# One op list for attention tail, mixing, transition and MLP, with the first block's LayerNorm inside the mixing

## The chip, the cores and the metric

The kernel runs on one core of one Trainium2 chip. Times are device microseconds of one execution, from the first instruction to the last on that core, with inputs and outputs in device memory. The profile is one execution of the same program, taken by the hardware profiler; its engines are PE (TensorE matmul), PEld (TensorE weight load), DVE (VectorE), ACT (ScalarE), POOL (GpSimd) and SP (SyncE, which here issues most DMAs).

## The reference

Three stages over batch 8, sequence 576, model width 512 (8 heads of 64).

```
phi(x)  = exp(+-(x @ w_phi - max|x @ w_phi|))                    # 2 x 128 features
attn    = phi(q) (phi(k)^T v) / (phi(q) sum_s phi(k) + 1e-6)      # per head, not causal
x       = attn, heads side by side                               # [8, 576, 512]
gate    = sigmoid(sum_k conv_w[k] * x[s - 4 + k])                 # 5 taps, causal
x2      = (gate * (x @ w_val)) @ w_out
u       = x2 + Re(FFT over width of (FFT over sequence of x2))
un      = (u - mean(u)) / sqrt(var(u) + 1e-6)                     # over width
out     = u + relu(un @ w_ch1) @ w_ch2                            # 512 -> 2048 -> 512
```

All in float32; each matmul is done as three matmuls of rounded high and low parts ("hi" and "lo"), and the two matrices of the MLP in a seven-product scheme (sums and differences of quarter blocks), whose sums of weight blocks are formed in the kernel and kept in a scratch array, `w_scr`.

## The kernel before

**Attention** is written by hand as steps (`run_attention`, L1281): step st projects piece st of q and k, and later stages of earlier pieces follow at fixed lags. Its last pieces end with a chain DVE `xs` (the normalised output), PE transposes `xt` (L336), ACT copy `xT`, a store to `x_scr` and a load of `xf`, one [512, 576] array for each batch. In the last steps (L1339 to L1342) the first batch's value products, `emit_V(0, m)` for four column chunks m, are written in.

**Mixing** goes batch by batch (L1359 to L1382), in the order in which the framework's scheduler puts it. For each batch: `split_x` (L433) makes hi on ACT and lo on POOL of the input (`xh`); `emit_V` (L465) makes a chunk: four tap multiply-adds on DVE (`acc`), sigmoid on ACT, 24 matmuls `val`, gating on DVE, the even and odd parts `gs`, hi on ACT and lo on POOL (`ge`). `emit_W` (L493) multiplies by w_out (`x2p`, 96 matmuls a batch), forms `fs` and its hi (ACT) and lo (DVE). `emit_FD` (L522) is the transform over width (tables `ft`, 39 matmuls), `emit_SD` (L563) the one over the sequence (tables `sq`, `sr`, 30 matmuls); its sums go into a tile `eo`, and from that DVE makes one half of u and POOL the other, and SP stores u to `u_scr`. Value products of batch b+1 run between the output products of batch b. `sum_w` (L359) loads weight blocks, forms their sums on POOL and stores them.

**The transition.** The last V chunk of batch 7 ends the written mixing. What is left of batches 6 and 7, the first MLP weights (`wr`, split into `w`), the LayerNorm of the first block (`ln_stages`, L767: sums `s`, `mean` by a matmul of ones, `A` minus mean, squares `T`, square root, reciprocal, `A` times `s`) and the MLP operands `un` are noted as ops (`note_last`, L1066) with the whole MLP (`note_mlp`, L1105).

**The planner.** `place_ops` (L1147) takes the noted ops with their dependences, gives each a duration from a small cost table, a due time from the order of the matmuls, and lets the ready op with the earliest due time go first on each engine. An op marked "vp" goes to DVE or POOL, whichever the planner finds free in time. Ops are marked old, any or new: tiles of the mixing are closed after the last old op and those of the MLP's first products (`x0`, `y`, `z`, `c11`, ...) opened after it, so that no MLP product runs before the last op of batch 7. All planned instructions carry line L59, that of the helper through which they are issued, as do the hi and lo splits and matmuls of the written part.

Of the kernel before, what the change touches and what calls it, by code (L numbers as in the profile page):

```python
# [1 line left out]

# [44 lines left out]
def resolve(x):  # L47
    return x.get() if isinstance(x, Late) else x
# [14 lines left out]
def attention_moe_mixer_kernel(  # L63
# [73 lines left out]

    base = pool(ctx, "base", 1)
# [38 lines left out]
    R = "right"  # L177
    wv_p = pool(gx, "wv", 1, side=R)
# [180 lines left out]
    def sum_w(n):  # L359
        for k in ((0, 1) if n == 0 else (n + 1,)):  # L360
            if k < len(wsteps):
                i, j, o = wsteps[k]
                wsum[k] = t = P["ws"].tile([128, 512], F32, tag="ws", name="ws")
                nc.sync.dma_start(out=t, in_=w_scr[i][j, o][:, 0:512])
        i, j, o = wsteps[n]
        t = wsum.pop(n)
        a21, a11, a12, a22 = (t[:, k * 128:(k + 1) * 128] for k in range(4))
        tt = nc.gpsimd.tensor_tensor
        tc.keep_in_program_order(tt(out=a22, in0=a21, in1=a22, op=ALU.add))
        tt(out=a21, in0=a11, in1=a21, op=ALU.subtract)  # L370
        tt(out=a11, in0=a22, in1=a11, op=ALU.subtract)
        tt(out=a12, in0=a12, in1=a11, op=ALU.subtract)
        nc.sync.dma_start(out=w_scr[i][j, o][:, 512:1024], in_=t)
# [26 lines left out]
    def open_mix():  # L400
        P["g0"] = pool(gx, "g0", 1, side=R)
        P["ws"] = pool(vx, "ws", 2, side=R)
        P["psv"] = pool(vx, "psv", 2, PSUM, side=R)
        P["psa"] = pool(vx, "psa", 1, PSUM, side=R)

    def open_mix2():
        P["x2"] = pool(mx, "x2", 1)
        P["fs"] = pool(mx, "fs", 1)
        P["ps"] = pool(mx, "ps", 4, PSUM)
        one = pool(mx, "one", 1)  # L410
        P["xr"] = [one.tile([128, NE], F32R, name=f"xr{i}") for i in range(2)]
        P["rem"] = [one.tile([128, NL], F32R, name=f"rem{a}") for a in range(2)]
        P["c256"] = one.tile([128, 5, 128], F32R, name="c256")
        P["r256"] = one.tile([97, 2, NE], F32, name="r256")
        for t in (*P["xr"], *P["rem"], P["c256"], P["r256"]):
            nc.gpsimd.memset(f32(t), 0.0)

    wsteps = [(i, j, o) for j in range(NJ) for i in range(2) for o in range(2)]
    wsum = {}
    xf = {}  # L420
    xhl = {}
    geo = {}
    x2 = {}
    fhl = {}
    yhl = {}

    def load_x(b):
        t = P["xf"].tile([128, 4, S + 4], F32, tag="xf", name="xf")
        nc.vector.memset(t[:, :, 0:4], 0.0)
        nc.sync.dma_start(out=t[:, :, 4:], in_=x_scr[b].rearrange("c p s -> p c s"))  # L430
        xf[b] = t

    def split_x(b, chunks=range(4)):  # L433
        if b not in xhl:
            xhl[b] = tuple(P["xh"].tile([128, 4, S], F32R, tag=f"x{i}", name="xh") for i in range(2))
        h, l = xhl[b]
        for c in chunks:
            hi_act(h[:, c], xf[b][:, c, 4:])
            lo_pool(l[:, c], xf[b][:, c, 4:], h[:, c])

    taps = {}

    def tap_steps(b, m):
        x = xf[b]
        if "psa" in P:
            acc = P["psa"].tile([128, 2, 512], F32, tag="pa", name="acc")[:, :, 0:HS]
        else:
            acc = P["g"].tile([128, 2, HS], F32, tag="acc", name="acc")

# [12 lines left out]
    def emit_taps(b, m):
        drain(tap_steps(b, m))

    def emit_V(b, m):  # L465
        h, l = xhl[b]
        if m == 0:
            geo[b] = tuple(P[f"g{b % 2}"].tile([128, 4, 2, NE], F32R, tag=f"g{i}", name="ge") for i in range(2))
        if (b, m) not in taps:
            emit_taps(b, m)  # L470
        t = taps.pop((b, m))
        acc = P["g"].tile([128, S], F32, tag="sg", name="sg")
        nc.scalar.activation(out=acc.rearrange("p (a s) -> p a s", a=2), in_=t, func=ACTF.Sigmoid)
        gv = P["g"].tile([128, NE], F32, tag="gv", name="gv")
# [12 lines left out]
        hi_act(gh[:, m], gs)
        lo_pool(gl[:, m], gs, gh[:, m])
        if m == 3:
            xhl.pop(b)  # L490
            xf.pop(b)

    def emit_W(b, c):  # L493
        gh, gl = geo[b]
        if b not in x2:
            x2[b] = P["x2"].tile([128, 4, 2, NE], F32, tag="x2", name="x2")
            fhl[b] = tuple(P["x2"].tile([128, 2, 2, NE], F32R, tag=f"f{i}", name="fh") for i in range(2))
        t = x2[b]
        for a in range(2):
            p = P["ps"].tile([128, NE], F32, tag="ps", name="x2p")  # L500
            for kk in range(4):
                ws = slice(c * 128, (c + 1) * 128)
                mm3(p, (wo[0][:, kk, ws], wo[1][:, kk, ws]), (gh[:, kk, a], gl[:, kk, a]), kk == 0, kk == 3)
            nc.scalar.activation(out=t[:, c, a, :], in_=p, func=ACTF.Copy)
            if c == 2 and a == 0:
                r = P["xr"][b % 2]
                hi_act(r[0:1, :], p[0:1])
                lo_dve(r[32:33, :], p[0:1], r[0:1, :])
            if c >= 2:
                if a == 0:  # L510
                    fs = P["fs"].tile([128, 2, NE], F32, tag="fs", name="fs")
                nc.vector.tensor_tensor(out=fs[:, a], in0=t[:, c - 2, a], in1=p, op=(ALU.add, ALU.subtract)[a])
# [972 lines left out]
```

## Time and profile before

| | us |
|---|---|
| median of three runs | 1389.01 (1388.45 to 1394.43) |
| profiled execution | 1393.84 |
| its span | 1391.9 |
| attention, up to 316.5 | 316.5 |
| attention tail, to 356.3 | 39.8 |
| mixing, batches 0 to 5 and the last V and W chunks, to 589.3 | 233.0 |
| transition, to the last sequence product | 44.7 |
| to the first MLP block's full pace at 658.9 | 24.9 |
| rest of the MLP | 733.0 |

The stages are cut where the trace's matmuls change name. Read it by stage: in each, the share of PE's busy time tells whether the matrix engine or something else sets the pace; the mean over the whole span hides this. Idle time in brackets behind an instruction is that of its engine just before it, with what released it.

### The profile page before, as it was taken

The page shows a single profiled execution, that of the slowest core. Times are in us where ns is not written, and L with a number is a line of the kernel's source. Part 1 is how long each engine was busy: PE and PEld are TensorE (multiplying, and loading weights), DVE is VectorE, ACT ScalarE, POOL GpSimd, SP SyncE. Part 2 cuts the span into 40 slices and gives each one's busy share as a digit, 9 for nine tenths or more (in the row PEclk, how much of TensorE's full clock was granted, in tenths as well). Part 3 has the DMA queues.
Part 4 walks back from the last instruction along what each step waited for, and adds up shares of the span by engine and source line. Part 5 has one row for each costly group of instructions (what it writes and reads, how often), then busy time and mean ns, then how long its engine had stood idle before and what let it go on. Part 6 is the DMA issues. An engine that isn't in the chain of part 4 may idle for free.

```text
span 1391.9 us, 35060 instructions
## 1 busy us (share of the span) xinstructions
PE 1335.0 (96%) x14672; PEld 1293.5 (93%) x14672; DVE 1177.5 (85%) x1989; ACT 816.8 (59%) x1549; POOL 609.0 (44%) x475
## 2 busy tenths in 40 slices
PE   7999999997999999977999999999999999999998
PEld 6888888987999999967999999999999999999998
DVE  6999998885889898788899999999888778777776
ACT  6888888863555545474555555655565455444542
POOL 3978888612577667533542243442313111111110
PEclk9999999998999999987999999999999999999999
DMA  6477877640344343245423233222533122222211
GB/s 244 156 276 261 280 265 259 223 166 26 107 152 158 134 142 111 88 161 204 131 85 121 92 121 101 89 91 86 167 115 118 63 68 84 89 64 91 91 48 45
DMA packets 89851, 186.98 MB, mean 134 GB/s; under 512 B 10455, under 2 KB 37335, under 8 KB 87518
## 3 DMA queue, kind: packets, MB, share of 16 engines
q1 hardware_dynamic: 88488, 181.33, 38.2%
q10 hardware_dynamic: 1206, 3.41, 0.6%
q8 instruction: 115, 1.88, 0.5%
q14 instruction: 42, 0.34, 0.1%
HBM read 121.79 MB, written 62.93 MB: 133 GB/s over the span
## 4 chain that ended last, share of the span: by engine, by line
PE 73%; DVE 15%; POOL 3%; issue 3%; ACT 3%; DMA 2%; SPq 0%; ACTq 0%; DVEq 0%; POOLq 0%
PE x L59 14%; PE cx L59 13%; PE y L59 7%; PE cy L59 6%; PE val L59 5%; PE x2p L59 5%; PE kv L59 4%; PE cz L59 4%; PE pj L59 3%; PE z L59 3%; PE nm L59 3%; DVE y L244 2%; PE yt L294 2%; DVE m L241 2%; DVE s L59 2%
## 5 line engine op out<-in xcount | busy, mean ns | idle before, releaser
L59 PE MATMUL cx<-h,w 128*128 128x256 f32 x1260 | 173.6, 284 | 0.0
L59 PEld LDWEIGHTS cx<-h,w 128*128 128x128 f32 x1260 | 161.9, 192 | 0.4 <-DVE acc L59 0.2
L59 DVE TENSOR_TENSOR acc<-cx,acc 128x512 f32<-128x512 f32 x144 | 99.0, 688 | 36.6 <-PE cx L59 35.7
L59 POOL TENSOR_TENSOR un<-A,un 128x512 fp32r<-128x512 f32 x38 | 49.2, 1302 | 173.2 <-ACT un L59 169.6
L59 PE MATMUL x<-un,w 128*128 128x256 f32 x864 | 118.0, 287 | 4.4 <-ACT c L59 2.3
L59 PE MATMUL val<-xh,wv 128*128 128x290 f32 x768 | 119.4, 305 | 1.3 <-DVE gv L481 0.6
L59 ACT ACTIVATE h<-z 128x512 fp32r<-128x512 f32 x108 | 64.4, 597 | 93.5 <-DVE z L59 92.8
L454 DVE SCALAR_TENSOR_TENSOR acc<-xf,cw,acc 128x576 f32<-128x576 f32 x128 | 105.1, 821 | 13.5 <-ACT acc L452 12.3
L59 PE MATMUL cy<-h,w 128*128 128x256 f32 x792 | 115.1, 282 | 1.2 <-DVE h L59 1.2
L59 PEld LDWEIGHTS x<-un,w 128*128 128x128 f32 x864 | 110.9, 195 | 5.1 <-ACT c L59 2.8
L59 PEld LDWEIGHTS val<-xh,wv 128*128 128x128 f32 x768 | 110.4, 195 | 3.2 <-POOL xh L59 1.4
L59 PEld LDWEIGHTS cy<-h,w 128*128 128x128 f32 x792 | 105.0, 191 | 1.4 <-DVE h L59 1.4
L59 PE MATMUL kv<-vraw,ke 128*64 128x66 f32 x2560 | 96.3, 228 | 3.1 <-DMA vraw<-in_v_dram 1.5
L59 PEld LDWEIGHTS kv<-vraw,ke 128*64 128x64 f32 x2560 | 84.0, 140 | 14.5 <-ACT qe L297 1.6
L241 DVE TENSOR_REDUCE m<-pj 128x8 f32<-128x1024 f32 (+1 forms) x80 | 88.6, 1107 | 9.6 <-PE pj L59 9.6
L59 POOL TENSOR_TENSOR un<-T,un 128x512 fp32r<-128x512 f32 x40 | 52.9, 1323 | 99.6 <-ACT un L59 99.6
L59 PE MATMUL x2p<-ge,wo 128*128 128x290 f32 x672 | 95.2, 296 | 0.0
L59 PE MATMUL pj<-wp,kqraw 64*128 64x128 f32 x1152 | 89.0, 292 | 5.5 <-DMA kqraw<-in_k_dram 4.4
L59 PEld LDWEIGHTS x2p<-ge,wo 128*128 128x128 f32 x672 | 91.8, 189 | 0.0
L59 PEld LDWEIGHTS pj<-wp,kqraw 64*128 64x128 f32 x1152 | 73.4, 193 | 19.1 <-issue 18.9
L244 DVE TENSOR_TENSOR y<-pj,m 128x1024 f32<-128x1024 f32 (+1 forms) x80 | 88.7, 1108 | 0.4
L59 PE MATMUL nm<-kvT,qe 128*64 128x65 f32 x2304 | 84.0, 225 | 4.8 <-DVE xs L323 2.7
(217 smaller groups left out, 3568.1 us busy)
## 6 DMA issues: line engine op xcount, KB each, us to landing
raw<-in_w_ch_dram SPq DMA_DIRECT2D x16, 1024.0 KB, 5.1
wr<-w_scr SPq DMA_DIRECT2D x32, 448.0 KB, 4.0
vraw<-in_v_dram SPq DMA_DIRECT2D x16, 660.0 KB, 9.1
x_scr<-xT SPq DMA_DIRECT2D x32, 288.0 KB, 2.8
xf<-x_scr SPq DMA_DIRECT2D x8, 1152.0 KB
out_dram<-acc SPq DMA_DIRECT2D x36, 256.0 KB, 2.2
kqraw<-in_k_dram SPq DMA_DIRECT2D x15, 576.0 KB
kqraw<-in_q_dram SPq DMA_DIRECT2D x15, 576.0 KB, 9.4
```

The lines of the kernel that those rows point to most:

```text
L59: return lambda *a, **k: f(*(resolve(x) for x in a), **{n: resolve(x) for n, x in k.items()})
L241: nc.vector.tensor_reduce(out=m, in_=pv, axis=AX.X, op=ALU.max, apply_absolute_value=True)
L244: nc.vector.tensor_tensor(out=y, in0=pv, in1=m.unsqueeze(3).to_broadcast([128, 2, 2 * n, F]), op=ALU.subtract)
L294: nc.tensor.transpose(t[:, h, j, :], y[:, h, n + j, :], ident)
L454: nc.vector.scalar_tensor_tensor(out=acc, in0=shifted(t), scalar=cw[:, m, t:t + 1], in1=acc, op0=ALU.mult, op1=ALU.add)
```

## The change

The last pieces of attention, the whole mixing, the transition and the MLP are now noted as one list of ops, and the planner places all of it. The two phases become five stages 0 to 4, each of which closes some pools of tiles and opens others; every key (tile) has a first and a last stage, and an op's stage follows from the keys that it reads and writes. The tiles of the MLP's first products (`x0`, `y`, `mean`, `c11`, `c12`, `c22`, the weights `w0`, `un`) open with stage 3, beside the last batches, where five PSUM banks go round for the mixing (six before).

```diff
     def run_attention():
...
-            for st in range(TOT + 6):
+            for st in range(TOT + 1):
...
-                if 1 <= st - TOT < 5:
-                    emit_V(0, st - TOT - 1)
...
+            note_mix()
+            note_mlp()
+            place_ops()
...
+    STAGES = {k: (a, b) for a, b, n in (
+        (0, 0, "early"), (0, 1, "att tr nm"), (0, 2, "xf xh sg"), (1, 2, "pv pa gv gs ws ge0"), (1, 3, "ge1"),
+        (2, 3, "x2 f Y fs u u256 xr rem c256 r256 ps T0 sh0 sl0"), (3, 4, "mean w0 sh sl T wr un c11 c12 c22 x0 y"),
+        (4, 4, "x1 z cx cy cz h acc w1"),
+    ) for k in n.split()}
```

The LayerNorm of the first block needs u of batch 0 alone; its load and its ops are now noted after batch 4. It takes its own tiles `T0`, `sh0`, `sl0`, and its mean a bank of the mixing's ring. Its last step, `prep_un(0)`, is noted at the end of the mixing.

```diff
+    def note_mix():
...
+        tail = note_tail()
+        next(tail)
+        for m in range(4):
+            note_taps(0, m)
+            note_V(0, m)
+            next(tail, None)
+        for b in range(NB - 1):
+            note_x(b + 1)
+            for i, c in enumerate((0, 2, 1, 3)):
+                if i < 3:
+                    note_taps(b + 1, i)
+                    note_V(b + 1, i)
+                note_W(b, c)
+                add_sums(1)
...
+            note_FD(b)
+            note_SD(b)
+            if b == 4:
+                load_a(0, u_scr)
+                ln_stages(0, K["ln0"])
+        b = NB - 2
         drain(prep_w(0, 0, K["w0"]))
         drain(prep_w(0, 1, K["w0"]))
-        ln_stages(0, K["ln0"])
-        phase[0] = "old"
-        note_FD(b, f, y, ring)
-        note_W(b + 1, geo[b + 1], xb, f, ring)
-        note_SD(b, x2[b], y, ring)
...
+        note_FD(b)
+        for c in (0, 2, 1, 3):
+            note_W(b + 1, c)
+        note_SD(b)
+        drain(prep_w(0, 2, K["w"]))
+        note_FD(b + 1)
+        note_SD(b + 1)
         prep_un(0, K["un0"])
```

In the mixing the engines of some ops change: the lo of `xh`, of `ge` and the weight sums may go to DVE or POOL (before: POOL); the lo of `fs` goes to POOL (before: DVE); the sums of the sequence products are formed in place in `x2`, so that there is no `eo`; both halves of u may go to either engine (before: one each); u is stored by ACT's queue (before: SP's in the written mixing).

```diff
-            lo_pool(l[:, c], xf[b][:, c, 4:], h[:, c])
+                o_lo("vp", l, x, h, S, [("xf", b % 2), ("xh", c, 0)], [("xh", c, 1)])
-        lo_pool(gl[:, m], gs, gh[:, m])
+        o_lo("vp", gl, gs, gh, 2 * NE, gk + [("ge", g, m, 0)], [("ge", g, m, 1)])
-        tt(out=a21, in0=a11, in1=a21, op=ALU.subtract)
+        o_tt("vp", a21, a11, a21, ALU.subtract, 128, [k11, k21], [k21])
-            lo_dve(fl[:, c0], fs, fh[:, c0])
+            o_lo(K["t_lo"], f[1][:, c0], fs, f[0][:, c0], 2 * NE, fk + [("f", c0, 0)], [("f", c0, 1)])
```

`K["t_lo"]` is "p" (POOL) as before; only the last batch used it then.

On DVE at the first block's LayerNorm, before: reciprocals, the product `A` times `s`, the low operands `un`, then the sums `eo` of batch 6.

```order
L59 RECIPROCAL s_9173<-s_9173 128x128
L59 TENSOR_TENSOR A<-A,s_9173 128x2x256 x4
L59 TENSOR_TENSOR T_9177<-A 128x512
L59 TENSOR_TENSOR T_9179<-A 128x512
L59 TENSOR_TENSOR un_1_9183<-A,un_0_9182 128x512
L59 TENSOR_TENSOR un_1_9185<-A,un_0_9184 128x512
L59 TENSOR_TENSOR un_1_9191<-T_9177,un_0_9190 128x512
L59 TENSOR_TENSOR un_1_9187<-A,un_0_9186 128x512
L59 TENSOR_TENSOR T_9177<-A,T_9177 128x512
L59 TENSOR_TENSOR wg_9201<-wr_9180,wg_9201 128x896
L59 TENSOR_TENSOR un_1_9193<-T_9177,un_0_9192 128x512
L59 TENSOR_TENSOR eo<-x_8880,ps_9205 128x290 x2
```

Now, at the same `un` operands of block 0 (here the reciprocals and the product `A` times `s` stand far above, among batch 6's ops): `un`, the differences `fs` of batch 7 (`x2b` is its array), then the sums of batch 6, in place in `x2` (here `x_6103`).

```order
L62 TENSOR_TENSOR un_1_8871<-T_8856,un_0_8870 128x512
L62 TENSOR_TENSOR un_1_8865<-T_8854,un_0_8864 128x512
L62 TENSOR_TENSOR fs<-x2b,ps_6123 128x290
L62 TENSOR_TENSOR fs<-x2b,ps_6124 128x290
L62 TENSOR_TENSOR wg_8872<-wr_8855,wg_8872 128x896
L62 TENSOR_TENSOR x_6103<-x_6103,ps_8831 128x2x290
L62 TENSOR_TENSOR x_6103<-x_6103,ps_6121 128x290 x2
L62 TENSOR_TENSOR x_6103<-x_6103,ps_6122 128x2x290
L62 TENSOR_TENSOR x_6103<-x_6103,ps_6123 128x290 x2
L62 TENSOR_TENSOR wg_8873<-wr_8857,wg_8873 128x896
```

The reciprocals and products have left this place; `fs` of batch 7 and the sums of batch 6 come right behind the operands.

On PE at the end of the mixing, before: the last sequence products of batch 7 (`sq`, `sr`) come ahead of the first MLP product, `x` from `un` and `w`.

```order
L59 MATMUL ps_9204<-sq,Y 128x290 x6
L59 MATMUL ps_9204<-sr,rem_6025 128x290
L59 MATMUL ps_9205<-sq,Y 128x290 x6
L59 MATMUL ps_9205<-sr,rem_6024 128x290 x2
L59 MATMUL ps_9206<-sq,Y 128x290 x6
L59 MATMUL ps_9206<-sr,rem_6025 128x290
L59 MATMUL x_9649<-un_0_9182,w_0_0_0_9169 128x256
L59 MATMUL x_9649<-un_1_9183,w_0_0_0_9169 128x256
L59 MATMUL x_9649<-un_0_9182,w_0_0_1_9170 128x256
```

Now the first MLP product (`x_8839`) stands between batch 6's sequence products and the width transform (`ft`) of batch 7; here its last rows.

```order
L62 MATMUL x_8839<-un_1_8859,w_1_0_0_8845 128x256
L62 MATMUL x_8839<-un_0_8858,w_1_0_1_8846 128x256
L62 MATMUL x_8839<-un_0_8858,w_1_1_0_8847 128x256
L62 MATMUL x_8839<-un_1_8859,w_1_1_0_8847 128x256
L62 MATMUL x_8839<-un_0_8858,w_1_1_1_8848 128x256
L62 MATMUL ps_6124<-ft_140,f_6109 128x258
L62 MATMUL ps_6124<-ft_141,f_6109 128x258
L62 MATMUL ps_6124<-ft_140,f_6115 128x258
```

One product of the MLP, 12 matmuls, has moved ahead of batch 7's two transforms.

On POOL in the attention tail, before: the lo of the first batch's input, the clearing of the mixing's small tiles, and four more lo of the next batch's input behind three lo of `ge`.

```order
L59 TENSOR_TENSOR xh<-xf,xh 128x576 x4
L416 MEMSET xr_6022 128x290
L416 MEMSET xr_6023 128x290
L416 MEMSET rem_6024 128x258
L416 MEMSET rem_6025 128x258
L416 MEMSET c_6026 128x640
L416 MEMSET r_6027 97x580
L59 TENSOR_TENSOR ge<-gs,ge 128x580 x3
L59 TENSOR_TENSOR xh<-xf,xh 128x576 x4
L59 TENSOR_TENSOR ge<-gs,ge 128x580 x2
L369 TENSOR_TENSOR ws<-ws 128x128
```

Now, at the lo of the next batch's input: weight sums (`ws`), two lo of `ge`, and two lo of the input.

```order
L62 TENSOR_TENSOR ws_5767<-ws_5767 128x128
L62 TENSOR_TENSOR ws_5763<-ws_5763 128x128
L62 TENSOR_TENSOR ws_5767<-ws_5767 128x128
L62 TENSOR_TENSOR ge<-gs,ge 128x580 x2
L62 TENSOR_TENSOR xh<-xf,xh 128x576 x2
L62 TENSOR_TENSOR ws_5763<-ws_5763 128x128
```

Two of the next batch's four `xh` have left POOL, and weight sums stand ahead of them.

On DVE in the attention tail now, at the gating of the first batch's last chunks (before, DVE had no `xh` and no `ge`):

```order
L62 COPY val_5768<-gv 128x1
L62 SCALAR_TENSOR_TENSOR acc<-xf,cw,acc 128x2x288
L62 TENSOR_TENSOR gs<-gv,val_5768 128x290 x2
L62 TENSOR_TENSOR xh<-xf,xh 128x576 x2
L62 TENSOR_TENSOR ge<-gs,ge 128x580
L62 SCALAR_TENSOR_TENSOR acc<-xf,cw,acc 128x2x288 x2
L62 TENSOR_TENSOR gv<-val_5764,acc 128x290
L62 SCALAR_TENSOR_TENSOR acc<-xf,cw,acc 128x2x288
```

The two `xh` that left POOL, and one `ge`, have moved here, between the taps (`acc`) and the gating.

## Rows read from the trace of the kernel before

**Rows 1.** The page's line of busy time, share of the span and instructions.
```profile
PE 1335.0 (96%) x14672; PEld 1293.5 (93%) x14672; DVE 1177.5 (85%) x1989; ACT 816.8 (59%) x1549; POOL 609.0 (44%) x475
```

**Rows 2.** Stretches: us, PE, PEld, DVE, ACT, POOL busy (x), PEclk, DMA share, GB/s.
```profile
316.50:356.30 39.80, 30.20 (x275) 28.01 (x275) 24.27 (x54) 15.78 (x28) 13.48 (x14) 0.79 0.16 53
356.30:589.30 233.00, 231.98 (x1745) 229.85 (x1744) 202.62 (x384) 119.83 (x260) 156.08 (x191) 1.00 0.36 127
589.30:634.00 44.70, 34.84 (x251) 33.33 (x249) 38.63 (x72) 28.87 (x63) 15.72 (x9) 0.89 0.46 152
634.00:658.90 24.90, 16.03 (x102) 15.15 (x102) 20.25 (x39) 13.62 (x25) 8.27 (x6) 0.81 0.61 219
700.00:1391.90 691.90, 683.14 (x5701) 681.23 (x5699) 575.08 (x920) 366.43 (x659) 173.53 (x144) 1.00 0.28 91
```

**Rows 3.** Timeline, PE, tail: start, us, instructions, [idle before <-releaser].
```profile
342.94 3.49 PE L59 MATMUL val<-xh,wv 128*128 128x290 f32 x24
349.01 0.41 PE L336 MATMUL xt<-ident,xs 128*128 128x128 f32 x2 [2.57 <-ACT xh L59]
350.00 6.45 PE L59 MATMUL val<-xh,wv 128*128 128x290 f32 x24 [0.59 <-DVE gv L481]
```

**Rows 4.** Timeline, POOL, tail.
```profile
347.28 5.53 POOL L59 TENSOR_TENSOR xh<-xf,xh 128x576 fp32r<-128x576 f32 x4 [1.70 <-ACT xh L59]
```

**Rows 5.** DVE by line, 460 to 589: xcount | busy, mean ns | idle before.
```profile
L581 DVE TENSOR_TENSOR u<-eo 128x578 f32<-128x578 f32 x8 | 11.2, 1412 | 0.0
L59 DVE TENSOR_TENSOR fh<-fs,fh 128x580 fp32r<-128x580 f32 x8 | 8.7, 1085 | 0.9 <-ACT fh L59 0.9
```

**Rows 6.** POOL by line, 357 to 589.
```profile
L59 POOL TENSOR_TENSOR ge<-gs,ge 128x580 fp32r<-128x580 f32 x27 | 39.4, 1459 | 54.6 <-ACT ge L59 54.5
L59 POOL TENSOR_TENSOR xh<-xf,xh 128x576 fp32r<-128x576 f32 x24 | 33.9, 1437 | 0.1
L369 POOL TENSOR_TENSOR ws<-ws 128x128 f32<-128x128 f32 x32 | 19.6, 612 | 2.2 <-DMA ws<-w_scr 2.2
L582 POOL TENSOR_TENSOR u<-eo 128x574 f32<-128x574 f32 x12 | 18.5, 1550 | 11.6 <-DVE eo L577 8.4 <-DVE val L482 3.2
```

**Rows 7.** SP's queue, 357 to 589: us in total, times, longest.
```profile
SPq L364 <- DMA w_scr<-ws: 68.6, 30, 5.4
```

**Rows 8.** Timeline, PE, transition.
```profile
585.95 3.40 PE L59 MATMUL val<-xh,wv 128*128 128x290 f32 x24
625.56 2.95 PE L59 MATMUL ps<-ft,fh 128*128 128x258 f32 x12 [8.65 <-DVE eo L59]
633.66 0.29 PE L59 MATMUL ps<-sr,rem 128*128 128x290 f32 x1
636.02 2.93 PE L59 MATMUL x<-un,w 128*128 128x256 f32 x12 [2.07 <-DVE r L59]
```

**Rows 9.** Timeline, DVE, transition.
```profile
596.98 1.43 DVE L59 TENSOR_TENSOR s<-s,A 128x256 f32<-128x256 f32 x4
601.33 1.28 DVE L59 TENSOR_TENSOR A<-A,mean 128x512 f32<-128x512 f32 x2
613.39 1.75 DVE L59 RECIPROCAL s<-s 128x128 f32<-128x128 f32 x2
616.53 2.43 DVE L59 TENSOR_TENSOR A<-A,s 128x512 f32<-128x512 f32 x4
632.11 2.09 DVE L59 TENSOR_TENSOR u<-eo 128x578 f32<-128x578 f32 x3
641.67 2.77 DVE L59 TENSOR_TENSOR u<-eo 128x578 f32<-128x578 f32 x4 [3.56 <-DMA u_scr<-u]
```

**Rows 10.** Timeline, ACT, transition.
```profile
610.10 1.28 ACT L59 ACT_TABLE_LOAD   x1
611.39 0.47 ACT L59 ACTIVATE s<-mean,eps 128x256 f32<-128x256 f32 x1
643.13 0.68 ACT L59 ACTIVATE u<-u 1x576 f32<-1x576 f32 x1 [11.88 <-DVE u L59]
```

More of the change, by code (lines that the diff above doesn't have):

```diff
@@ L177, in attention_moe_mixer_kernel @@
     R = "right"
+    ln_p = pool(lx, "ln", 1, side=R)
+    late["s1"] = ln_p.tile([128, TB], F32, name="s1")
+    late["A"] = ln_p.tile([128, 4, TB], F32, name="A")
     wv_p = pool(gx, "wv", 1, side=R)
@@ L418, in attention_moe_mixer_kernel @@
-    wsteps = [(i, j, o) for j in range(NJ) for i in range(2) for o in range(2)]
[L419 to L425, printed above, removed]
+        p = pool(gx, "g0", 1, side=R)
+        ws = pool(vx, "ws", 1, side=R)
+        psv = pool(vx, "psv", 1, PSUM, side=R)
+        psa = pool(vx, "psa", 1, PSUM, side=R)
+        for g, q in enumerate((p, P["g1"])):
+            for i in range(2):
+                late["ge", g, i] = q.tile([128, 4, 2, NE], F32R, tag=f"g{i}", name="ge")
@@ L462, in emit_taps, with split_x @@
[L462 to L474, printed above, removed]
+    def split_x(c):
+        if c == 0:
+            for i in range(2):
+                late["xh", i] = P["xh"].tile([128, 4, S], F32R, tag=f"x{i}", name="xh")
+        h, l = late["xh", 0], late["xh", 1]
+        x = late["xf", 0][:, c, 4:]
+        hi_act(h[:, c], x)
+        lo_pool(l[:, c], x, h[:, c])
@@ new lines, in note_taps @@
+    def note_taps(b, m):
+        t, s = later(("xf", b % 2)), later(("sg", m % 2))
+        xk, sk = ("xf", b % 2), ("sg", m % 2)
+        first = b == 0 and m < 2
+        acc, k = (s, sk) if first else (later("pa")[:, :, 0:HS], "pa")
+        if b or m:
+            o_act(acc, shifted(t, m, 4), ACTF.Copy, S, [xk], [k], scale=cw[:, m, 4:5])
+            for i in range(4):
+                op("v", S, lambda e, i=i: vec.scalar_tensor_tensor(
+                    out=acc, in0=shifted(t, m, i), scalar=cw[:, m, i:i + 1], in1=acc, op0=ALU.mult, op1=ALU.add
+                ), [xk, k], [k], two=True)
+        o_act(s, acc, ACTF.Sigmoid, S, [k], [sk])
@@ L695, in op @@
             dur = {e: dur}
-        ops.append((dur, fn, reads, writes, more, two, phase[0]))
+        at = [stage(k) for k in reads + writes]
+        ops.append((dur, fn, reads, writes, more, two, max([a for a, b in at], default=0), min([b for a, b in at], default=4)))
     def o_hi(dst, src, cols, r, w):
@@ L1150, in place_ops @@
         pred = [set() for _ in range(n)]
-        for i, (d, f, r, w, more, two, ph) in enumerate(ops):
+        for i, (d, f, r, w, more, two, lo, hi) in enumerate(ops):
             for k in r:
@@ L1192, in place_ops @@
         end = [0.0] * n
-        before = [o[6] == "old" for o in ops]
+        part = [o[6] for o in ops]
+        last = [o[7] for o in ops]
         for i in reversed(range(n)):
-            if before[i]:
-                for p in pred[i]:
-                    before[p] = True
-        after = [o[6] == "new" for o in ops]
-        shut = set()
-        open_old = {e: sum(1 for i in range(n) if before[i] and e in ops[i][0]) for e in "mvapd"}
+            last[i] = min([last[i]] + [last[j] for j in succ[i]])
+            assert part[i] <= last[i], ops[i][2:4]
+        left_by = {e: [0] * 5 for e in "mvapd"}
+        for i in range(n):
+            for e in ops[i][0]:
+                left_by[e][last[i]] += 1
+        at_part = dict.fromkeys("mvapd", 0)
         def first(i, e):
```

690 lines of the change are left out of this document (316 added, 374 removed).

## The prediction

> **What bounds the kernel now.** I read the page's first line, then the stretches by stage, then the timelines of PE, POOL, DVE and ACT where PE idles. By the first line PE is busy for 96% [rows 1], which would leave 57 us to gain. The stretches show where they lie [rows 2]. In the mixing PE is busy 231.98 of 233.00 us, in the MLP 683.14 of 691.90: no order of the same matmuls can gain more than 1.0 us in the one, and the other is hardly touched. Two stretches are open: the tail, 9.6 us idle of 39.8 at a granted clock of 0.79, and the transition with the MLP's start, 9.9 of 44.7 and 8.9 of 24.9 at 0.89 and 0.81. Together 28.4 us, and what the lower clock costs beside.
>
> In the tail, PE waits 2.57 us ahead of 349.01, and then for the next batch's V. Its input's high and low parts lie in one buffer, so the lows begin behind the value products of 342.94, and the four POOL lows of 347.28 take 5.53 us, to 352.81 [rows 3, 4]. The 24 products of that V take 6.45 us from 350.00, against 3.49 for the same number before [rows 3]; the first output products follow at 356.29.
>
> In the transition, DVE bounds: it is busy 38.63 of 44.7 us [rows 2], with the first block's LayerNorm among it [rows 9], and PE waits 8.65 us for the sums `eo` ahead of the last 12 of batch 7's width matmuls; the sequence products end at 633.95, and the first MLP product begins only at 636.02 [rows 8]. Behind it stands a chain through one tile: u of batch 6 is complete at 632.11 + 2.09 = 634.2, its store must leave before u of batch 7 is written at 641.67 [rows 9], ACT's copy into that u waits 11.88 us at the head of ACT's queue, to 643.13 [rows 10], and the copies `c` that let PE go on are queued behind it.
>
> **The change part by part.**
>
> Tail. The chain of the last attention pieces stays as it is. Of the next batch's four lows, two now go to DVE. A low of about this size costs DVE 1.09 us [rows 5] and POOL 1.38 [rows 4]; two on each side by side end at 347.28 + 2.8 = 350.1, 2.7 us sooner, and some of the slow 6.45 us goes too. Against this, ACT alternates between exponential and sigmoid, two table loads more, at 1.28 us each [rows 10], beside waits of a few us on PE. I take -3.0. Bounds: 0, if the gating of the last chunk is late as well and then ends the wait; -8, if nearly all of the 9.6 us idle goes.
>
> Mixing, engines. DVE is busy 202.62 of 233 us, POOL 156.08 [rows 2]. With some 34 us a batch, DVE loses two lows of `fs` (2 x 1.09) and perhaps one half of u, and gets some lows of `xh` and `ge`; it stays near 30 of 34. POOL gets the lows of `fs`, about 1.46 each [rows 6]; a wait of PE on them is new: behind such a low stand weight sums and `ge`, and the width products wait for it. By the order its slack is about 1 us. PE cannot gain here. Bounds of this exchange alone: 0, and +2 by the MLP's share, 98.7% busy under the same planner against 99.6% now [rows 2]. I take +1.5.
>
> Mixing, LayerNorm. On DVE stand four reciprocals of 0.88, four subtractions of 0.64, four products of 0.61, and some nine of the sixteen sums and lows at 0.36 (POOL may take the rest) [rows 9]: 3.5 + 2.6 + 2.4 + 3.2 = 11.7 us. Two batches with 4.5 us of idle DVE each take 9 of it; 2.7 are over. Its square root costs two more table loads on ACT, 2.6 us, which is busy for half of the stretch [rows 2], so they are covered unless a sigmoid waits. I take +2.5. Bounds: 0, if it fits, and +8, if two thirds of it delay the gating.
>
> First what the row shows: a table load takes 1.28 us and the square root starts 0.01 us behind it [rows 10]. The Trainium skill (ScalarE: Activation LUTs, What ACT_TABLE_LOAD costs) puts 1.38 us of drain beside the load, 2.66 us a switch. By the rows the four loads more cost ACT 5.1 us, by the Trainium skill 10.6; the difference is ACT time that has cover, and the trace shows no such drain behind the load.
>
> Two engines side by side can also cost: DVE's half of u takes 1.41 us beside POOL's half of 1.55 [rows 5, 6], and 0.69 where POOL does none (2.77 for four) [rows 9]. Every low that moves from POOL to DVE while POOL works may pay such a 0.7. The Trainium skill (GPSIMD Engine Reference, 1. Specifications) says that the two engines share the memory ports when a DVE instruction has two inputs there; the trace agrees, with those two durations.
>
> Transition. From the end of batch 7's last V (T0 = 589.35 [rows 8]) PE has the remaining products of batches 6 and 7, 39 + 96 + 30 + 39 + 8 + 30 = 242, and now two MLP products of 12 among them: 266. At the mixing's pace, 231.98 / 1745 = 0.133 us [rows 2], 35.4 us, where the stretch took 44.7. DVE's 38.63 us lose the LayerNorm's 11.7 and leave 27, so PE becomes the bound. Up to the sums of batch 6 stand 39 + 96 + 30 + 12 = 177 products, 23.5 us, and DVE's low operands `un`, `fs` of batch 7 and the six sums come about then, some 5 us, and u itself, 2.1: complete at T0 + 31 to 33, where it was at T0 + 44.9. The store, u of batch 7, ACT's copy and `c` follow as before, at the same length, so the MLP gets its pace that much sooner: -12.4. About 1 goes to new waits, since the first weights `wr` and batch 7's `x2b` lie where batch 7's input was and can only be written after T0. I take -11.5. Bounds: -6, if PE's 35.4 us and 3.5 us of waits go ahead of u; -17, if DVE does its 27 us unbroken and a part of the clock comes back.
>
> The MLP behind it stays: 0, bounds -1 and +1, the same ops under the same costs.
>
> Sum: -3.0 + 1.5 + 2.5 - 11.5 = -10.5. The profiled execution took 1393.84 us, of which 1391.9 span; it would take 1383.3. It lies 4.8 us above the median of the runs, so for those I say 1389.01 - 10.5 = 1378.5.
>
> **The rivals.**
>
> A. The LayerNorm only moves. The mixing's DVE has few holes, and its 11.7 us and the collisions with POOL delay the gating of batches 5 to 7: mixing +9 instead of +4. For it speaks DVE's 87% in the mixing; against it that PE had only 1.0 us of waits there, so some queue of ready products exists. -3.0 + 9 - 11.5 = -5.5: 1383.5.
>
> B. The chain through u's one tile stays late: DVE does the operands `un` and `fs` of batch 7 ahead of batch 6's sums, and u of batch 6 is complete at T0 + 40 only. For it speaks the order of DVE, where these stand in this row; against it DVE's load, 27 of 35 us. The transition then gives 4: -3.0 + 4 - 4 = -3, 1386.0.
>
> C. Slower: POOL holds up PE in every batch. The lows of `fs` stand behind weight sums that wait for their load, and each load waits for the store before it: 68.6 / 30 = 2.3 us each time, at most 5.4 [rows 7]. Now POOL only loses 2.2 us there [rows 6], and nobody waits for it. If such a wait falls ahead of one low of `fs` in each of 7 batches and 3 us of it exceed the slack, PE loses 21 us; the sum is +10.5, 1399.5. It decides from 10.5 / 7 = 1.5 us a batch on.
>
> D. More: the tail gives 8, the LayerNorm costs nothing, the transition gives 17. -25, 1364.0. For it speaks that a PE without gaps also gets its full clock, 1.00 in the mixing, against 0.79 to 0.89 where it idles [rows 2]; against it that three terms must all be at their ends.
>
> **How the numbers follow.** My forecast 0.47, A 0.18, B 0.10, C 0.10, D 0.15. Of no change I speak within 0.5%, 6.9 us, about what a measurement can tell here: faster is below 1382.1. The forecast's own spread of 5 us leaves four fifths below that, a sixth in the band; A a third below, the rest in the band; B is in the band, C above it in four cases of five, D below. Faster 0.38 + 0.06 + 0.15, about 0.59; within 0.29; slower 0.12. The range holds the forecast, A, B and nearly all of D, and leaves out C: 1363 to 1393; the forecast's own is 1372 to 1385.
>
> **What the profile after would show.** Right: the stretch from the last V to the last sequence product takes 34 to 38 us instead of 44.7, with no wait of PE over 3 us on DVE; the table load for the square root stands in the mixing; V of batch 1 takes about 3.5 to 4.5 us for its 24 products; the mixing's PE stays above 97% busy. Wrong: if PE shows waits on POOL's low of `fs` in each batch (C), on gating in batches 5 to 7 (A), or if ACT's copy into u comes as long after T0 as now, 54 us (B). The tail's term is wrong if the first output products come less than 1 us sooner after the last attention piece.

## The result, and the profile after

The changed kernel takes 1378.82 us (median of five runs, 1377.72 to 1381.04), against a forecast of 1378.5. Its ratio to the kernel before, whose median beside it was 1394.04, is 0.991, with a 95% interval of 0.9893 to 0.9928: faster by 10 to 15 us. Its profiled execution took 1378.82 us, span 1377.0.

The first line of its page, as [rows 1]:

```profile
PE 1330.1 (97%) x14672; PEld 1288.3 (94%) x14672; DVE 1183.7 (86%) x2006; ACT 820.5 (60%) x1554; POOL 582.0 (42%) x452
```

The same matmuls, 14672 of them; DVE does a little more, POOL 27 us less. Where the time went is read by stage. The cuts are events of PE's timeline: attention ends where the last transposes `yt` ahead of the first `val` begin; the tail ends where the first output product (from `ge`, `wo`) begins; the mixing where batch 7's last V ends; the transition where the last sequence product ends; then up to the first product `cx`, and the rest. In us:

| | attention | tail | mixing | transition | to `cx` | rest | span |
|---|---|---|---|---|---|---|---|
| before | 315.7 | 40.6 | 233.1 | 44.6 | 27.7 | 730.3 | 1391.9 |
| before, second profile | 313.0 | 40.6 | 233.1 | 44.5 | 25.6 | 729.8 | 1386.5 |
| after | 312.3 | 39.8 | 234.5 | 35.9 | 27.3 | 727.2 | 1377.0 |
| after, second profile | 311.2 | 39.7 | 235.7 | 36.1 | 27.6 | 727.4 | 1377.6 |

The first column is not the change: attention runs the same instructions in both. Without it, the profiles shown differ by 1064.7 - 1076.2 = -11.5 us: -0.7 in the tail, +1.5 in the mixing, -8.7 in the transition, -0.4 up to `cx`, -3.1 behind it (some 1.6 of these, 12 matmuls at 0.133 us, because one more MLP product now runs ahead of that cut).

The stretches of the changed kernel, with the columns of [rows 2]:

```profile
312.27:352.10 39.83, 30.85 (x280) 27.72 (x280) 30.95 (x63) 20.65 (x33) 18.44 (x28) 0.83 0.32 106
352.10:586.63 234.53, 232.96 (x1754) 231.05 (x1753) 208.82 (x421) 125.43 (x271) 129.37 (x153) 1.00 0.37 126
586.63:622.49 35.86, 34.51 (x268) 33.91 (x268) 33.10 (x53) 23.62 (x55) 15.36 (x12) 1.00 0.47 155
622.49:649.81 27.32, 16.73 (x104) 15.43 (x104) 20.74 (x35) 16.24 (x28) 6.26 (x6) 0.75 0.53 182
649.81:1377.00 727.19, 717.91 (x5986) 715.48 (x5984) 606.92 (x969) 385.25 (x691) 191.69 (x155) 1.00 0.29 94
```

The transition is now full: PE is busy 34.5 of 35.9 us, at a granted clock of 1.00 (2.4 GHz) instead of 0.89. The stretch behind it is emptier than before: 10.6 us idle at 0.75, where it had 8.9 at 0.78.

PE's timeline in the tail, which answers to [rows 3]:

```profile
341.15 3.43 PE L62 MATMUL val<-xh,wv 128*128 128x290 f32 x13 [2.01 <-DVE gs L62]
345.24 0.66 PE L62 MATMUL val<-xh,wv 128*128 128x290 f32 x3 [0.66 <-POOL xh L62]
346.61 0.68 PE L62 MATMUL val<-xh,wv 128*128 128x290 f32 x3 [0.70 <-POOL xh L62]
348.06 4.20 PE L62 MATMUL val<-xh,wv 128*128 128x290 f32 x17 [0.78 <-DVE xh L62]
```

POOL's timeline there, which answers to [rows 4]:

```profile
343.78 2.78 POOL L62 TENSOR_TENSOR xh<-xf,xh 128x576 fp32r<-128x576 f32 x2
```

and DVE's:

```profile
346.33 0.82 DVE L62 TENSOR_TENSOR gs<-gv,val 128x290 f32<-128x290 f32 x2
347.07 1.87 DVE L62 TENSOR_TENSOR xh<-xf,xh 128x576 fp32r<-128x576 f32 x2
```

Ahead of the first row 84 of batch 0's 96 value products have run, so that 12 of its 13 are batch 0's too, and batch 1's begin with the thirteenth, at 344.1. Counted from the end of attention, V of batch 1 begins at 31.9 us instead of 34.3 and ends at 39.8 instead of 40.6. Its 24 products take 8.0 us instead of 6.3: the first two lows come one after the other on POOL, the other two stand on DVE behind the last chunk's taps and gating, and the last 17 products took 4.20 us, mostly at a granted clock of 0.50.

PE's timeline in the transition and behind it, as [rows 8]:

```profile
608.01 1.59 PE L62 MATMUL x<-un,w 128*128 128x256 f32 x12
...
617.21 1.01 PE L62 MATMUL ps<-sq,c 128*97 128x290 f32 x6 [1.24 <-DVE Y L62]
...
638.34 0.58 PE L62 MATMUL mean<-sh,ones 128*128 128x256 f32 x1 [7.62 <-ACT sh L62]
```

The wait of 8.65 us on `eo` is gone, and the longest up to the last sequence product is 1.24. Behind it a wait of 7.62 us has come up. ACT's timeline shows what stands behind it, as [rows 10]:

```profile
628.07 0.68 ACT L62 ACTIVATE u<-u 1x576 f32<-1x576 f32 x1 [2.76 <-DVE u L62]
...
629.93 0.95 ACT L62 ACTIVATE w<-wr 128x896 fp32r<-128x896 f32 x1 [1.18 <-DVE u L62]
635.99 0.95 ACT L62 ACTIVATE w<-wr 128x896 fp32r<-128x896 f32 x1 [5.12 <-DMA u_scr<-u]
...
637.89 0.40 ACT L62 ACTIVATE sh<-s 128x256 fp32r<-128x256 f32 x1
```

ACT writes a weight tile of the second matrix; that tile lies where u of batch 7 was, and must wait until u has been stored. The copy `sh` for which PE waits, and the MLP's `h`, are queued behind it.

The LayerNorm's square root on ACT, now in the mixing:

```profile
535.34 1.28 ACT L62 ACT_TABLE_LOAD   x1
536.64 0.47 ACT L62 ACTIVATE s<-ps,eps 128x256 f32<-128x256 f32 x1
...
540.42 1.28 ACT L62 ACT_TABLE_LOAD   x1
```

### The profile page after: what moved, and what is told of

The parts are those of the page before. It is cut to its first block, busy times and chain, and to the rows that moved or that the text cites. A ratio compares the mean times of both kernels' runs of the same rounds, so it can differ in the third digit from the quotient of the medians.

```text
span 1377.0 us, 35052 instructions
## 1 busy us (share of the span) xinstructions
PE 1330.1 (97%) x14672; PEld 1288.3 (94%) x14672; DVE 1183.7 (86%) x2006; ACT 820.5 (60%) x1554; POOL 582.0 (42%) x452
## 3 DMA queue, kind: packets, MB, share of 16 engines
q1 hardware_dynamic: 85312, 174.25, 37.7%
## 4 chain that ended last, share of the span: by engine, by line
PE 71%; DVE 21%; ACT 4%; issue 2%; DMA 1%; SPq 0%; POOL 0%; ACTq 0%; DVEq 0%
PE x L62 14%; PE cx L62 13%; PE ps L62 9%; PE cy L62 7%; PE y L62 7%; PE val L62 6%; PE cz L62 4%; DVE y L260 3%; PE z L62 3%; DVE m L257 3%; DVE acc L62 3%; PE kv L62 3%; PE pj L62 3%; PE nm L62 2%; DVE cv L126 2%
## 5 line engine op out<-in xcount | busy, mean ns | idle before, releaser
L62 DVE TENSOR_TENSOR acc<-cx,acc 128x512 f32<-128x512 f32 x144 | 98.8, 686 | 34.8 <-PE cx L62 34.1
L62 POOL TENSOR_TENSOR un<-A,un 128x512 fp32r<-128x512 f32 x41 | 55.1, 1353 | 172.8 <-ACT un L62 169.2
L62 PE MATMUL val<-xh,wv 128*128 128x290 f32 x768 | 115.7, 306 | 4.7 <-DVE gs L62 2.6
L62 PE MATMUL ps<-ge,wo 128*128 128x290 f32 x768 | 107.0, 297 | 0.6 <-ACT s L62 0.6
L62 PEld LDWEIGHTS ps<-ge,wo 128*128 128x128 f32 x768 | 104.2, 189 | 0.8 <-ACT s L62 0.8
```

Of the source, the lines that this page charges most:

```text
L62: return lambda *a, **k: f(*(resolve(x) for x in a), **{n: resolve(x) for n, x in k.items()})
```

## The experiments

Medians of runs; "against the changed kernel" is against 1380.92 us, its median when it ran again. The experiments ran on three occasions; the kernel before, run beside each, had medians of 1390.6, 1391.0 and 1391.1, so that the occasions differ by little. Stages are cut as in the table above.

**Once more, the changed kernel and the kernel before.**

> The changed kernel as it is, for comparison on the same chip. All theories: 1377 to 1381 us. If the 3.4 us by which its attention stage ran shorter than that of the kernel before come from the change (its pools or its instruction addresses), every profile shows attention's last common matmuls at about 310 us; if they are chance of the start, some profile of either kernel shows 313.

> The kernel before, profiled once more. Theory (the length of the attention stage differs by a few us between executions of the same code, and the later stages do not): its attention ends anywhere from 311 to 317 us, while tail, mixing, transition and the rest agree with its first profile within 1 us each: 40.6, 233.1, 44.6, 27.7 and 730.3. Rival (the kernel before has the longer attention, so the change gains there too): 315 to 316 again, and beside it no profile of a changed kernel at 315 or above.

Measured: the changed kernel 1380.92 us, ratio 0.9927 (0.9908 to 0.9946); the kernel before 1388.9 in its one run. The profiles are in the table: attention ended at 311.2 and 313.0 us, where the first profiles had 312.3 and 315.7; over all fourteen profiles of this study, whose attention is the same, it ended between 311.2 and 316.5 (both ends in kernels with the change or a variant of it). The rival falls: 3.4 us of the difference between the first two profiles is chance. Tail, mixing and transition repeat within 1.2 us; the stretch up to `cx` of the kernel before moved by 2.1, where the theory had 1.

**The LayerNorm late.**

```diff
             if b == 4:
-                load_a(0, u_scr)
-                ln_stages(0, K["ln0"])
...
         drain(prep_w(0, 1, K["w0"]))
+        load_a(0, u_scr)
+        ln_stages(0, K["ln0"])
         note_FD(b)
```

> Undoes one part: the first block's LayerNorm is noted behind the first weights, at the transition, as before; the rest of the change stays. Theory (the transition was bound by DVE, with the LayerNorm's 11.7 us in it): PE waits on DVE again ahead of batch 6's sums, the stretch from the last V to the last sequence product goes from 35.9 back to 41 to 45 us, the mixing gets its 1.5 us back, total +4 to +8 us against the changed kernel. Rival (the early MLP products and the early open tiles carry the gain): within +2 us.

Measured: 1408.74 us, ratio 1.0125 (1.0104 to 1.0145), +27.8 against the changed kernel and slower than the kernel before, which has its LayerNorm in the same place. Mixing 232.7, transition 61.3. Its waits on SP's queue (us in total, times, longest), and its PE:

```profile
SPq L657 <- PE val L62: 83.6, 1, 83.6
```

```profile
598.35 1.50 PE L62 MATMUL ps<-ft,f 128*33 128x258 f32 x6 [9.52 <-DVE Y L62]
601.16 3.19 PE L62 MATMUL ps<-ge,wo 128*128 128x290 f32 x12 [1.30 <-DVE rem L62]
605.97 0.99 PE L62 MATMUL ps<-ft,f 128*128 128x258 f32 x6 [1.38 <-DVE A L62]
```

Both my numbers failed. Two things beside DVE's work are in it. The load of u for the LayerNorm stands on SP's queue behind the first weights' loads, whose tiles lie where batch 7's input was, and those wait for its last V; the load then landed 6.96 us after its issue at 588.88, and DVE's sums waited for it ahead of the width transform's `Y`. And the mean's products take banks of the mixing's ring in turn, so that width products wait for the LayerNorm's `A` (twice 1.38 us).

```diff
             if b == 4:
                 load_a(0, u_scr)
-                ln_stages(0, K["ln0"])
...
         drain(prep_w(0, 1, K["w0"]))
+        ln_stages(0, K["ln0"])
```

> As the run with the LayerNorm noted late, but the load of its input u stays where the change puts it, after batch 4. In that run the load stood on SP's queue behind the first weights' loads, which wait for batch 7's last V (83.6 us), landed 6.96 us after T0, and DVE's first LayerNorm sums held up DVE for it; it came out 28 us above the changed kernel. Theory (the load's place made 20 of these 28 us, the LayerNorm's DVE work the rest): +5 to +10 us against the changed kernel, stretch from the last V to the last sequence product 41 to 46 us. Rival (the LayerNorm's ops at the transition cost it all, wherever the load is): +20 us or more.

Measured: 1407.44 us, ratio 1.012 (1.0097 to 1.0144), transition 61.6. It decides nothing: the load was noted early, but the planner still put it behind the weights' loads (issued at 586.83), presumably because nothing that needs it was due early.

Next, on top of this run, a bank of its own for the mean, and a key `a0` that the load of u writes and the weights' loads read:

```diff
-            b, p = ("mean", tl["mean"]) if t else next(ring)
+            b, p = ("mean", tl["mean"])
...
-            o_dma([(r, w_scr[i][j, o, :, 128:1024])], [("w_scr", i, j, o)], [("wr", b)], 448)
+            o_dma([(r, w_scr[i][j, o, :, 128:1024])], [("w_scr", i, j, o), "a0"], [("wr", b)], 448)
...
-              [("u_scr", b) for o, n, b, s in parts], AK, 1024)
+              [("u_scr", b) for o, n, b, s in parts], AK + ["a0"] * (t == 0), 1024)
```

> LayerNorm noted late again, with two side effects of the last two such runs taken away: its load of u is put ahead of the first weights' loads on SP's queue (there it had stood behind them, which wait for batch 7's last V), and its mean has a bank of its own instead of banks of the mixing's ring, whose order had tied the width products of batches 6 and 7 to the LayerNorm's steps. What is left is the LayerNorm's work on DVE at the transition. Theory (that work is worth what the prediction said, some 9 to 12 us of transition against 2 to 3 of mixing): +5 to +10 us against the changed kernel, the last V to the last sequence product 42 to 46 us. Rival (the LayerNorm's place alone costs the 26 to 28 us): +20 us or more.

Measured: 1392.75 us, ratio 1.0017 (1.0005 to 1.0029), +11.8 against the changed kernel, a little over the theory's range and far below the rival's. Transition 44.0, as before the change; mixing 233.0; up to `cx` 34.2. Its two stretches, columns as above:

```profile
584.88:628.87 43.99, 38.59 (x277) 37.10 (x276) 38.09 (x62) 28.52 (x64) 18.17 (x10) 0.92 0.36 121
628.87:663.10 34.23, 20.50 (x117) 18.97 (x116) 27.50 (x51) 16.42 (x31) 8.28 (x7) 0.70 0.57 195
```

DVE is busy 38.1 of 44.0 us, as in the kernel before (38.6), against 33.1 of 35.9 with the LayerNorm in the mixing. So its place is worth 8 us in the transition and 6.8 up to `cx`, and costs the mixing 2.2 (235.1, the mean of the two profiles, against 233.0). The other 16 us of the first two such runs were the load's place and the ring's banks; both were taken away at once, so their shares are not shown. With its ratio of 1.0017 this run is where the kernel before is: without the LayerNorm's place, the rest of the change gains nothing in sum.

**No MLP product early.**

```diff
-        (2, 3, "x2 f Y fs u u256 xr rem c256 r256 ps T0 sh0 sl0"), (3, 4, "mean w0 sh sl T wr un c11 c12 c22 x0 y"),
-        (4, 4, "x1 z cx cy cz h acc w1"),
+        (2, 3, "x2 f Y fs u u256 xr rem c256 r256 ps T0 sh0 sl0"), (3, 4, "mean w0 sh sl T wr un"),
+        (4, 4, "c11 c12 c22 x0 y x1 z cx cy cz h acc w1"),
```

> Undoes another part: the tiles x0, y, c11, c12, c22 of the first MLP products belong to the last stage, so that no MLP product runs before the mixing's tiles close; the LayerNorm stays in the mixing. Theory (the LayerNorm carries the transition's gain, the early products only fill PE): u of batch 6 is complete up to 3 us sooner, four to six products of 1.6 us come later, total 0 to +6 us against the changed kernel. Rival (the early products carry it): +8 us or more.

Measured: 1380.74 us, ratio 0.9929 (0.9909 to 0.9948), no difference from the changed kernel. Transition 34.1 and up to `cx` 26.0, but 731.5 behind it, against 727.2: what is not done early is done later at the same price. The rival falls.

**The lo of `fs` on DVE, and the lows of `xh` and `ge` on POOL alone.** One value (`t_lo="v"`), and in two places `"p"` for `"vp"`.

> The lo of fs goes back from POOL to DVE in all batches. Theory (POOL has slack, DVE some 4 us a batch): -1 to +2 us against the changed kernel, with no wait of PE on POOL's f either way. Rival C (POOL's lo of fs is late in each batch): -3 us or better.

> The lo of xh and of ge go back to POOL alone, as before the change. Theory (the choice of engine gained next to nothing in the tail, where V of batch 1 began 5.4 us sooner and ended only 0.8 us sooner): -1 to +2 us against the changed kernel. Rival (the two lows on DVE are what the tail gained, and POOL is too full without the choice): +3 us or more.

Measured: 1386.47 us, ratio 0.9966 (0.9951 to 0.9981), +5.6; and 1388.87, ratio 0.9978 (0.9959 to 0.9997), +8.0. The mixing takes 239.7 and 242.2 instead of 235.1. PE's waits in it (us in total, times, longest), all of the changed kernel's:

```profile
PE ps L62 <- POOL f L62: 0.6, 1, 0.6
PE ps L62 <- ACT s L62: 0.6, 1, 0.6
PE ps L62 <- DVE Y L62: 0.3, 1, 0.3
```

the two largest of the first of the two:

```profile
PE ps L62 <- DVE Y L62: 1.8, 2, 1.4
PE ps L62 <- DVE f L62: 0.8, 2, 0.5
```

and of the second, with DVE ahead of its longest one:

```profile
PE ps L62 <- DVE rem L62: 3.8, 3, 1.7
PE ps L62 <- POOL f L62: 1.9, 2, 1.0
```

```profile
525.94 3.29 DVE L62 TENSOR_TENSOR ws<-ws 128x128 f32<-128x128 f32 x3
```

Both moves of lows were needed: each undone costs the mixing 4 to 7 us, more than either theory said. The second one's rival (+3 or more) has the number, but not the place: the tail took 39.6 us, and the mixing grew. (The 5.4 us in that expectation took the first row of `val` above for batch 1's; it is 2.4.) My rival C is wrong as stated (the lo of `fs` on POOL holds PE up by 0.6 us in all, 1.2 in the second profile), and so is my estimate that the moves hardly matter. In the second run weight sums stand on DVE ahead of all three waits for `rem`: beside POOL's four lows (523.35 to 529.08) three took 3.29 us, where one alone took 0.28 to 0.29. Waits are not all of it: PE waits 3.6 and 6.3 us in the two, against 1.5 and 2.1 in two profiles of the changed kernel, and behind a wait the granted clock fell for a time, which it did in neither of these. In the first run it was 0.50 from 521.1 to 524.5, where 16 matmuls took 3.40 us; at the mixing's pace they take 2.1.

**Batch 1's lows on DVE.** `"v" if b == 1 else "vp"` for the lo of `xh`.

> Only in batch 1, all four lo of xh on DVE. Theory (V of batch 1 is held by the lows: two on POOL one after the other at 1.39 us, two on DVE behind the taps): V of batch 1 loses its waits of 0.66, 0.70 and 0.78 us and part of its run at the lower clock, -1 to -3 us against the changed kernel. Rival (the lows then delay the taps and the gating on DVE, or stand behind them): 0 to +2 us.

Measured: 1384.01 us, ratio 0.9949 (0.993 to 0.9968), +3.1 by medians; tail 40.7 us instead of 39.8, the later stages within 0.9 of the changed kernel's. The rival's mechanism holds; its 0 to +2 fits the tail's +0.9, not the +3.1, and the rest was not traced. PE and DVE:

```profile
349.26 5.18 PE L62 MATMUL val<-xh,wv 128*128 128x290 f32 x23 [3.32 <-DVE xh L62]
```

```profile
347.69 0.81 DVE L62 TENSOR_TENSOR gs<-gv,val 128x290 f32<-128x290 f32 x2
348.42 3.31 DVE L62 TENSOR_TENSOR xh<-xf,xh 128x576 fp32r<-128x576 f32 x4
```

DVE comes to the lows only after the last chunk's gating, at 348.42; the three waits on lows have become one.

**The second matrix's weight tiles in reverse order.**

```diff
-        for j in range(NJP):
+        for j in reversed(range(NJP)):
             late["w", 1, j] = w_tiles(big, 1, j)
```

> One line: the tiles of the second MLP matrix are laid out in reverse order, so that its first weights lie over tiles that are dead early and not over u, whose store takes 6.5 us. Theory (the hole of 7.6 us on PE before 638.3 in the changed kernel is ACT's weight copy, waiting for that store at the head of its queue, with the LayerNorm's sh and the h behind it): the hole shrinks by 3 to 5 us, total -3 to -5 us against the changed kernel. Rival (the loads of acc queued behind the store on the same memory are waited for by DVE for 4.8 us anyway): the wait moves to DVE, within 1 us.

Measured: 1376.84 us (1375.65 to 1382.79), ratio 0.9908 (0.9884 to 0.9932): -4.1 against the changed kernel by medians, though single runs overlap. Up to `cx` 23.9 us against 27.3 and 27.6. PE and ACT:

```profile
634.90 0.38 PE L62 MATMUL mean<-sh,ones 128*128 128x256 f32 x1 [2.62 <-ACT sh L62]
...
643.59 1.65 PE L62 MATMUL x<-un,wg 128*128 128x256 f32 x6 [3.61 <-ACT c L62]
```

```profile
631.71 1.79 ACT L62 ACTIVATE w<-wr 128x896 fp32r<-128x896 f32 x2 [1.17 <-DVE u L62]
...
640.77 0.95 ACT L62 ACTIVATE w<-wr 128x896 fp32r<-128x896 f32 x1 [1.31 <-DMA wr<-w_scr]
```

The wait of 5.12 us is gone, and PE's 7.62 has become 2.62. DVE's wait for loads of `acc`, 4.81 us in the changed kernel, is gone too, so the rival falls. What is late next is a load of weights. By its median this is the fastest version measured.

**The LayerNorm earlier.** On top of the last one, `if b == 2` and `if b == 3` for `if b == 4`.

> The second matrix's weight tiles moved (as in e6), and the first block's LayerNorm noted after batch 2 instead of 4, so that two more batches have room for it. Theory (the mixing's 2 to 3 us for the LayerNorm come from DVE being full in the two batches that take it): -1 to -2.5 us against e6. Rival (the planner puts it where it is due, late, wherever it is noted): within 1 us of e6.

> As the run before, but noted after batch 3. Theory: -0.5 to -2 us against e6. Rival: within 1 us of e6.

Measured: 1385.16 us, ratio 0.9961 (0.9942 to 0.998), and 1392.54, ratio 1.0009 (0.9996 to 1.0022): 8 and 16 slower than with the LayerNorm after batch 4. The mixing takes 242.7 and 249.7 us. Neither theory nor rival said so. In the second, one stretch and the wait in it:

```profile
480.00:520.00 40.00, 31.28 (x216) 29.87 (x216) 39.12 (x76) 19.89 (x36) 20.46 (x27) 0.96 0.37 130
```

```profile
501.26 6.52 PE L62 MATMUL val<-xh,wv 128*128 128x290 f32 x36 [5.07 <-DVE gv L62]
```

```profile
497.92 2.91 DVE L62 TENSOR_TENSOR s<-s,A 128x256 f32<-128x256 f32 x4
500.75 0.45 DVE L62 TENSOR_TENSOR gv<-val,acc 128x290 f32<-128x290 f32 x1
```

DVE is busy 39.1 of 40 us there, and the gating `gv` stands behind the LayerNorm's six sums, the last four of which took 2.91 us, part of the time beside POOL, against 1.43 before [rows 9]: this is rival A's mechanism, collision with POOL included. In the first of the two PE never waits for gating. Its longest wait, 2.62 us, is for ACT's `f`, and DVE's `fs` for that stood behind this:

```profile
519.74 0.53 DVE L62 TENSOR_TENSOR ws<-ws 128x128 f32<-128x128 f32 x1 [3.17 <-POOL ws L62]
```

A weight sum on DVE waited for its other half on POOL, and that 6.78 us for a load of `ws`; the LayerNorm was over by then (its last product `A` times `s` at 505). So that wait is rival C's mechanism, moved to DVE; the rest of this run's 7.0 us of waits was not traced. How thinly the LayerNorm is spread does not order the three: from its load to its last product it lies between 495 and 568 us in the changed kernel, between 393 and 505 in the first of these runs and between 485 and 553 in the second.

## Why the prediction was right, point by point

- **The sum** was -10.5; the profiles give -11.5 without attention's chance, the medians 10 to 15. That 1378.5 and 1378.82 lie so close is luck: 1389.01, from which I counted, became 1394.04 with two runs more, and from the profiled execution I had 1383.3.
- **The chances**: by the parts that I gave, "within" adds up to 0.32 and "slower" to 0.10, not to 0.29 and 0.12; "faster", 0.59, stands.
- **Transition**: right in mechanism, and nearly in size. I said -11.5; transition, start of the MLP and the rest together gave -12.2. PE became the bound (34.5 of 35.9 us), its wait on DVE went from 8.65 to 1.24, and the stretch lies within the 34 to 38 I had named. The run with the LayerNorm late and its side effects gone shows that DVE's work was the cause: 44.0 again. DVE was left with 33.1 us, though, and not with 27: eight weight splits stand in the stretch, 9.6 us, where six took 6.5, sums of the second block came in, and operations beside POOL took up to 1.78 us instead of 0.69.
- **The chain behind it** was the wrong step: "follow as before, at the same length". u of batch 6 was complete at 620.8, T0 + 34.1, not 31 to 33: two of its parts stood on POOL, with sums of the second block between them, and two on DVE among weight splits (rows below). From there to ACT's copy into u the chain was even shorter, 7.3 us against 8.9, since u of batch 7 shows no wait for the store, where it had 3.56 [rows 9]. But behind that copy a new link came in, the tile of the second matrix over u (5.12 us). Counted from T0, the change gave -10.7 at u of batch 6, -12.3 at ACT's copy and -9.1 at the first `cx`. The MLP behind `cx`, which I had at 0, gave 3.1, half of it a product moved ahead; the other half was not traced. That the two misses offset each other is luck. The parts of u on POOL, and then on DVE, with u of batch 7 last:

```profile
610.07 1.21 POOL L62 TENSOR_TENSOR u<-x 128x578 f32<-128x578 f32 x1 [0.18 <-DVE x L62]
...
616.37 1.18 POOL L62 TENSOR_TENSOR u<-x 128x574 f32<-128x574 f32 x1
```

```profile
617.32 0.84 DVE L62 TENSOR_TENSOR u<-x 128x578 f32<-128x578 f32 x1
...
619.01 1.08 DVE L62 TENSOR_TENSOR wo<-wr,wo 128x896 fp32r<-128x896 f32 x1
620.02 0.75 DVE L62 TENSOR_TENSOR u<-x 128x574 f32<-128x574 f32 x1
...
626.60 2.77 DVE L62 TENSOR_TENSOR u<-x2b 128x578 f32<-128x578 f32 x4
```

- **Mixing**: +4.0 (1.5 and 2.5) against +1.5 and +2.7 measured in two profiles; the LayerNorm's part, 2.2, was close to its 2.5. The exchange of engines, at +1.5, cost nothing: with the LayerNorm late the mixing took 233.0, as before the change. That the moved lows would be worth about nothing was wrong, since either of them undone costs 4 to 7 us while the LayerNorm is in the mixing. So the two terms seem to hang together, the room for the LayerNorm coming from the lows; no run undid a low with the LayerNorm late.
- **Tail**: -3.0 against -0.7, so the term is wrong by its own sign, and V of batch 1 took 8.0 us, not 3.5 to 4.5. The price of the lows was about right (DVE 0.93 and POOL 1.39 each), but they were not "on each side by side": DVE's order had taps and gating ahead of them, so that its two began at 347.07, after POOL's had ended. The other part is the granted clock, which the term left out: in three variants the same tail took 37.7 to 37.9 us, 2.7 to 2.9 less than before (last section).
- **Rivals**: A is no fiction; with the LayerNorm after batch 3 it happens, and the mixing takes +17 against the kernel before, where I priced +9 (after batch 2, +10, the longest wait had another cause). B did not come: u of batch 6 was complete at T0 + 34.1, not 40, and ACT's copy into u came 41.4 us after T0, not 54. C did not come: 0.6 to 1.2 us of waits on POOL's lo of `fs` in the whole mixing. D did not come either: tail -0.7, transition and MLP -12.2, and the LayerNorm was not free.
- **Table loads**: four more, two of them in the mixing. In the changed kernel the square root starts 0.02 us behind its load of 1.28, as before; the Trainium skill's drain (ScalarE: Activation LUTs, What ACT_TABLE_LOAD costs) shows again in no row here.

## What to carry to other kernels

Work that stands on a vector engine at a transition, and is needed only behind it, is worth moving into a stage where the matrix engine is the bound, but only as far as that stage's vector engines have room; its place within the stage decided between +2 and +17 us here, and the two earlier places failed for different reasons. A planner that knows dependences and not memory places loads ahead of what frees their tiles, and lays tiles over others that are stored late: after such a move read the queue's waits and ask of each first writer what its tile lay on. A predicted sum can be right while two of its terms are wrong, so compare by stage, and leave out a stage that the change doesn't touch. Of a stage with idle matrix engine read more than one profile, with the granted clock beside each.

## What the runs showed of the hardware

The attention stage, with the same instructions, ended between 311.2 and 316.5 us in fourteen executions. In the first two profiles a part of the difference was there from the start. The first 40 us of the kernel before, and of the changed one:

```profile
0.00:40.00 40.00, 32.45 (x567) 28.88 (x567) 28.00 (x41) 26.04 (x46) 17.51 (x11) 0.91 0.63 231
```

```profile
0.00:40.00 40.00, 33.30 (x595) 29.34 (x597) 30.25 (x43) 27.65 (x49) 19.24 (x12) 1.00 0.65 237
```

The granted clock was 0.91 and 1.00, and 28 matmuls more were recorded in the second.

The tail differs too, with the same instructions in the same order: in ten profiles (the changed kernel's two and those of the variants that leave the tail alone) it took 39.7 to 40.1 us where its mean granted clock was 0.83 (five), 38.8 at 0.87 (two) and 37.7 to 37.9 at 0.91 (three). The 13 value products at 341.15 above took 3.43 us at 0.52, nearly all of it at the lower level of 0.50 (1.2 GHz); in the run with the lo of `fs` on DVE the same 13 ran at 1.00 (2.4 GHz):

```profile
341.45 2.18 PE L62 MATMUL val<-xh,wv 128*128 128x290 f32 x13 [2.01 <-DVE gs L62]
```

What let the clock fall in one execution and not in another was not separated.

DVE's operand `un` beside POOL's and alone, in the transition of the changed kernel (POOL's two took from 594.99 to 598.35):

```profile
597.12 1.78 DVE L62 TENSOR_TENSOR un<-A,un 128x512 fp32r<-128x512 f32 x1
...
600.22 0.69 DVE L62 TENSOR_TENSOR un<-T,un 128x512 fp32r<-128x512 f32 x1
```

A subtraction of this shape took 1.78 us with POOL at work and 0.69 without; u had shown the same before the change [rows 5, 9].
